# Masks made by GpSimd, score tiles in runs, and a new order of the first loads in an attention and max-out kernel

## The chip, the cores and the metric

The kernel runs on one core of a Trainium2 chip. The metric is the device time of one execution in microseconds (us). Three timed runs of the kernel before gave 184.52, 184.63 and 184.64, so the median is 184.63.

## What is computed

There are 4 batches of 8 heads, 768 positions and 64 elements per head. The reference in short:

```python
scores = scale * np.matmul(q, k.transpose(0, 1, 3, 2))
stream_keep = causal & (is_sink | in_win)     # 4 sinks, window 64
mask = where(is_retrieval[head], causal, stream_keep)
a = softmax(where(mask, scores, -1e9))
x = matmul(a, v)                              # heads side by side: (3072, 512)
h1, h2 = x @ w1, x @ w2                       # (512, 1024) each
out = np.maximum(h1, h2) @ w_out              # float32
```

Three of the eight heads see the whole causal triangle ("F"), five see only the sinks and the window ("S"). Which heads these are is data: the kernel reads the flags, sorts the heads and addresses them through registers.

## The kernel before, in words

The work is cut into 4 batches of two halves with 384 queries each, named (b, hf). Heads go in four pairs p: one FF, one FS and two SS.

For each half the stages are these. q, k and v are loaded as float32 by SyncE's queue (`load_half`, lines L513 and L523) into one of three large slots (`lds`). ScalarE, VectorE and GpSimd cast q and k to bf16 (`cast_qk`, helper lines L480 and L482). TensorE turns them (`turn`, L712), and a copy takes the result to SBUF (`unturn`). TensorE makes score tiles of two PSUM banks each (`scores`, L893). ScalarE takes the exponentials of each bank (`exp`, L912) into one of `NAT` = 6 tiles of weights. VectorE multiplies by 0/1 masks (`mask`, L931). TensorE multiplies the weights with v (`weighted`, L956), and VectorE divides by the row sums (`normalise`, L973 and L983). For the stream heads, `mix_k` and `mix_v` lay the sinks beside the window. The half (0, 0) differs: its masks come in as a bias of 0 or -1e30, added by a matmul with the identity ahead of the scores (L867, at most two in each score tile), so it needs no mask on VectorE.

max(h1, h2) is computed as relu(x(w1 - w2)) + x w2. So w1 - w2 goes to `w12` (VectorE, L1122, four column blocks c), and w2 w_out is made once: `P` turns w2 (L1138) and `P2` multiplies by w_out (L1156). P2 is 16 groups of two matmuls, named by block c and bank kc. Group c needs block c of w2, turned and copied out, and piece c of w_out, which GpSimd's queue loads and casts (L616). Each half then has eight `up` steps U (L1177, relus L1201 or L1203), each of four matmuls of 384 columns, and three output tiles D of twelve matmuls of 512 columns (L1227), which are copied out and stored by SyncE's queue (L1244). Batch 3 is loaded and cast by GpSimd's DMAs (L569) and turned by DMA (L583).

The order of the work is not written out by hand. A planner (class `Order`) plays the whole kernel through at build time with a cost for each operation, a rank for each kind (`RANK`), a minimum wait for some TensorE lists (`MARGIN`) and due times, and emits every engine's instructions in the order that it finds. On the chip each engine then follows this fixed order and waits on semaphores. TensorE takes from its lists in the order TX, W, S, TQ, P, H, P2, F. Where nothing is ready early on, the planner emits dummy matmuls on a zeroed tile (L471) to keep the clock up.

In the fixed order of before, SyncE's queue issues q and k of (0, 0), the bias table from HBM (L595, 256 KB), v of (0, 0), q and k of (0, 1), the four blocks of w2, v of (0, 1), the four blocks of w1, then batch 1. ScalarE's queue loads the flags (L1474) and the identity (L1558, 32 KB). VectorE makes the 0/1 tables from the bias table (L646). Score tiles are issued in fixed pairs (`TOGETHER`).

Of the kernel before, what the change touches and what calls it, by code (L numbers as in the profile page):

```python
# [39 lines left out]
def one(p, hh, blocks):  # L40
# [72 lines left out]
TOGETHER = (  # L113
    [[0, 1], [2, 3], [4, 5], [6]], [[0, 1], [2, 3], [4, 5], [6, 7], [8, 9]],
    [[0], [1], [2], [3], [4], [5]],
)
# [20 lines left out]
class Order:  # L137
# [6 lines left out]
    def __init__(self, banks, dummy, dummies_until):  # L144
        self.ops, self.lists, self.n, self.shift = [], {}, 0, 0.0
        self.banks, self.freed = [None] * banks, [0.0] * banks
        self.at, self.dummy, self.dummies_until = {}, dummy, dummies_until
# [41 lines left out]

    def run(self, names, allowed):  # L190
# [11 lines left out]
        rings, served = {"SP": [], "POOL": []}, [0.0, 0]  # L202
# [16 lines left out]
        def begin(o, e, t):  # L219
            cost = o.costs[e]  # L220
# [53 lines left out]
        left = len(self.ops)  # L274
        while events:
# [25 lines left out]
            while again:  # L301
# [20 lines left out]
                for relaxed in (False, True):  # L322
                    chosen = None
                    for n in names:
# [10 lines left out]
                        if o.claims and self.place(o.claims, False, SPARE.get(n, 0)) is None:  # L335
                            continue
                        chosen = n, o
                        break
                    if chosen:
# [4 lines left out]
                        begin(o, "PE", t)  # L344
                        again = True
                        break
                else:
                    if t < self.dummies_until:
                        spot = self.place([("dummy", 1)], False)
                        last = 0.107 if t < COLD_UNTIL else 0.056  # L350
                        if spot and (t < COLD_UNTIL or used(t) < WARM_SHARE):
                            self.dummy(spot["dummy"][0])
                            done_pe.append((t, t + last, 1.0))
                        if spot:
                            free["PE"] = t + last
                            push(t + last, None)
# [7 lines left out]
REGISTERS = 4.4  # L364
TURNED_BY_PE = (0,)
# [3 lines left out]
    'cast': 3.05, 'vcast': 13.85, 'unturn': 4.05, 'mix_k': -0.7, 'mix_v': -14.35, 'exp': 4.1,  # L369
    'mask': -5.1, 'norm': -4.75, 'take_x': -8.75, 'turn': 8.65, 'w2b': 9.4, 'sub': -4.6, 'w2t':  # L370
    -8.95, 'wob': -4.45, 'w2o': -10.4, 'relu': -0.25, 'load': 10.7, 'out': -0.6, 'h2': 7.85,
    'table': -2.75, 'vload': -2.25,
# [5 lines left out]
NAT = 6  # L378
# [19 lines left out]
W2O_EARLY = 3  # L398
# [3 lines left out]
DMA_LATE = {'SP': 2.7, 'POOL': 3.2}  # L402
RING = 4224
SPLIT = ((0, 0),)
K_BY_ACT = False
K_LANDS = 7.6
# [13 lines left out]
MARGIN = {'W': 2.0, 'S': 0.8, 'F': 2.0, 'TQ': 0.8}  # L420
X_MARGIN = 1.5


def tile_three_full_heads(
    tc, q, k, v, w1, w2, wo, out, tab, table_dram, heads, rez, found, verdict, warm, early_k, lds
# [18 lines left out]
    NLD, NQB, NQK, NMIX, NAT, NX, NXT, NG, NOUT = 3, 4, 8, 6, 6, 2, 4, 2, 4  # L444
# [33 lines left out]
    def copy(e, out, in_):  # L478
        if e == "ACT":
            nc.scalar.copy(out=out, in_=in_)  # L480
        else:
            eng[e].tensor_copy(out=out, in_=in_)  # L482

# [22 lines left out]
    def load_half(b, hf, kinds=(0, 1, 2)):  # L506
# [33 lines left out]
        if (b, hf) == (0, 0) and 0 in kinds:  # L540
            order_.insert(2 if long else 2 * NT, (3, 0))
        for t, i in order_:
# [3 lines left out]
            if t == 3:  # L546
                bias_in.append(load_table(128, 1152))
            elif t < 2 and long:
# [45 lines left out]
    def load_table(lo, hi):  # L594
        return dma(0.262, lambda _: nc.sync.dma_start(  # L595
            out=tab[:, lo:hi], in_=table_dram.ap()[:, lo:hi]
        ), rate=0.4, parts=128, grain=85.0)

# [25 lines left out]
    for what in LOADS:  # L624
        kind, c = what[:2], int(what[2:]) if what[:1] == "w" else 0
        if what[0] in "AB":
            kinds = (2,) if what[1:] else (0, 1)
            load_half(0, "AB".index(what[0]), kinds)
            flow += loads[0, "AB".index(what[0]), kinds[-1]]
# [6 lines left out]
    registers = order.given(REGISTERS)  # L636

# [143 lines left out]
    def prepare(b, hf, p):  # L781
# [7 lines left out]
        else:  # L789
# [4 lines left out]
            for hh in range(2):  # L794
                for lo, hi in ((0, 1), (1, 2)) if (b, hf) in SPLIT else ((0, 2),):
# [3 lines left out]
                        tag=f"cast{b}.{hf}.{p}", rank=RANK["cast"], port=("DVE", "POOL"),  # L799
# [9 lines left out]
            for hh in range(2) if b not in V_BY_DMA else ():  # L809
                vs.append(op(  # L810
                    dict(CAST_V), cast_v(n, hf, hh), [*loads[b, hf, 2], registers, *old_v],
                    tag=f"vcast{b}.{hf}.{p}", rank=RANK["vcast"], port=("POOL", "DVE"), bias=BIAS if b else None,
# [10 lines left out]
            else:  # L823
# [4 lines left out]
                    frees=[key], tag=f"unturn{b}.{hf}.{p}", rank=RANK["unturn"],  # L828
# [3 lines left out]
        if "S" in kind and (b or hf):  # L832
# [11 lines left out]
            for what in range(2) if hf == 0 or late else (1,):  # L844
                cols = 64 * (NT if hf else NT - 1 if what else 2 * NT - 1)
                ks.append(op({"DVE": 0.07 + cols / 1920}, mix_k(n, hf, what), [un, *firsts, *olds], tag=f"mixk{b}.{hf}.{p}", rank=RANK["mix_k"], port=("DVE",)))
                cols = VW * wide * (NT if hf else NT - 1 if what else 2 * NT - 1)
                vmix.append(op({"DVE": 0.045 + cols / 2400, "POOL": 0.25 + cols / 1200, "ACT": act(cols)}, mix_v(n, hf, what), [*vs, *vfirsts, *oldw], tag=f"mixv{b}.{hf}.{p}", rank=RANK["mix_v"], port=("POOL", "DVE"), bias=BIAS_MIX))
# [145 lines left out]
    def attend(b, hf):  # L994
        group = group_of(b, hf)
        exps, done = {}, {}
        for together in TOGETHER[2 if (b, hf) == (0, 0) else hf]:
            deps = []
            cost = 0.19
            for t in together:  # L1000
                blocks = [x_ for bk in group[t][0] for x_ in bk]
                for p, hh, blk in blocks:
# [6 lines left out]
                heads_ = [{(p, hh) for p, hh, _ in bk} for bk in group[t][0]]  # L1009
                serial = all(h[1] == 0 for s_ in heads_ for h in s_)  # L1010
                cost += mm(*[128] * len(group[t][0][0])) * (2 if serial else 1)
                cost += mm(*[128 * m * times for _, _, m, _, times in biases(b, hf, t)])
# [601 lines left out]
```

## Time and profile before

| | us |
|---|---|
| median of three timed runs | 184.63 |
| the profiled execution | 184.92 |
| its span, first to last instruction | 182.0 |
| TensorE busy, as the page counts it | 171.5 |
| ScalarE busy | 131.6 |
| VectorE busy | 96.7 |
| GpSimd busy | 42.4 |

The profiled execution is 2.9 us longer than its span, and 0.3 us longer than the median. TensorE's clock was granted at 0.998 of full speed. Matmuls are pipelined and their ends are modelled, so the busy time of TensorE contains overlaps: a group of 8 U matmuls is listed with 1.46 us, while the next group starts 1.3 us after it. Distances between starts are therefore used as costs, not the durations.

### The profile page before, as it was taken

To read this page: it belongs to the slowest core of one execution; us is meant where nothing else is said; L and a number is where in the kernel's file an instruction comes from. 1 tells how busy PE (TensorE), PEld (TensorE's weight loads), DVE (VectorE), ACT (ScalarE), POOL (GpSimd) and SP (SyncE) were. 2 spreads that over 40 slices of the span, in tenths; PEclk is the share of its full clock that TensorE was granted. 3 is DMA by queue.
4 is the path that set the end of the run, shared out by engine and by line. 5 is a ranking of instruction groups with operands and counts; after the bars stand their busy time and mean duration, and the time that the engine had idled before them with its cause. 6 is when DMAs were issued, how large, how long until landed. Compare 5 with 4: busy or idle time off the path is not lost.

```text
span 182.0 us, 4932 instructions
## 1 busy us (share of the span) xinstructions
PE 171.5 (94%) x1836; PEld 105.3 (58%) x1836; DVE 96.7 (53%) x283; ACT 131.6 (72%) x287; POOL 42.4 (23%) x77
## 2 busy tenths in 40 slices
PE   7599599989999999999999999999999999999991
PEld 7567486466647656565545565565466545545560
DVE  3356896599689984576247476656447500000000
ACT  3399794596899999999996984777797524525430
POOL 1000810100609489899580000000000000000000
PEclk9999999999999999999999999999999999999999
DMA  4999999999899999999999994160151052012022
GB/s 136 323 242 339 347 223 244 349 290 280 221 290 270 326 294 295 160 243 202 179 140 147 248 177 118 63 144 0 61 144 61 0 144 115 11 58 115 0 99 87
DMA packets 74930, 32.68 MB, mean 180 GB/s; under 512 B 54162, under 2 KB 71826, under 8 KB 74898
## 3 DMA queue, kind: packets, MB, share of 16 engines
q1 hardware_dynamic: 54848, 28.84, 62.4%
q0 software_dynamic: 19904, 3.41, 25.4%
q8 instruction: 16, 0.26, 0.6%
q14 instruction: 16, 0.13, 0.2%
q10 hardware_dynamic: 146, 0.03, 0.1%
HBM read 25.46 MB, written 6.29 MB: 174 GB/s over the span
## 4 chain that ended last, share of the span: by engine, by line
PE 64%; SPq 11%; DMA 9%; DVE 5%; ACT 4%; issue 2%; POOL 2%; POOLq 0%; DVEq 0%; ACTq 0%
PE ps L1227 30%; PE ps L1177 20%; DMA ld<-in_v_dram 6%; PE ps L956 6%; PE ps L893 6%; SPq L523 5%; SPq L608 3%; DMA ld<-in_q_dram 3%; DVE w L1122 2%; SPq L513 2%; PE ps L712 2%; ACT at L912 2%; ACT qk L480 1%; POOL qb L482 1%; DVE at L931 1%
## 5 line engine op out<-in xcount | busy, mean ns | idle before, releaser
L912 ACT ACTIVATE at<-ps 128x512 bf16<-128x512 f32 (+2 forms) x134 | 65.1, 601 | 3.5 <-PE ps L893 1.9
L1227 PE MATMUL ps<-wob,g 128*128 128x512 bf16 (+1 forms) x200 | 46.8, 371 | 0.2 <-ACT at L912 0.2
L1177 PE MATMUL ps<-xt,w 128*128 128x384 bf16 x256 | 46.0, 326 | 0.9 <-DVE w L1122 0.7
L1177 PEld LDWEIGHTS <-w 128*128 128x128 bf16 x256 | 23.6, 97 | 15.9 <-issue 0.9
L931 DVE TENSOR_TENSOR at<-at,tab 128x1024 bf16<-128x1024 bf16 (+5 forms) x49 | 25.6, 538 | 13.3 <-ACT at L912 13.0
L1201 ACT ACTIVATE g<-ps 128x384 bf16<-128x384 f32 x56 | 27.5, 504 | 7.0 <-PE ps L1177 6.5
L1227 PEld LDWEIGHTS <-g 128*128 128x128 bf16 x200 | 18.2, 98 | 17.8 <-issue 0.4
L480 ACT COPY ot<-ps 128x512 f32<-128x512 f32 (+1 forms) x20 | 11.4, 572 | 22.8 <-PE ps L1227 22.6
L1227 PE MATMUL ps<-w2o,xt 128*128 128x512 bf16 (+1 forms) x100 | 24.8, 371 | 0.3 <-ACT qk L480 0.3
L956 PEld LDWEIGHTS <-at 128*128 128x128 bf16 x477 | 19.9, 97 | 7.3 <-issue 0.2
L983 DVE TENSOR_TENSOR x<-ps,rez 128x192 f32 x64 | 22.8, 356 | 1.8 <-DVE x L983 0.2
L956 PE MATMUL ps<-vb,at 128*128 128x65 bf16 x387 | 21.6, 193 | 0.0
L482 POOL CAST qb<-ld 128x384 bf16 x23 | 12.1, 561 | 35.6 <-DMA ld<-in_k_dram 35.6
L893 PE MATMUL ps<-qk 64*128 64x128 bf16 (+1 forms) x322 | 20.2, 230 | 0.0
L893 PEld LDWEIGHTS <-qk 64*128 64x128 bf16 x322 | 12.0, 94 | 11.2 <-issue 8.2
L1227 PEld LDWEIGHTS <-xt 128*128 128x128 bf16 x100 | 9.2, 98 | 9.0 <-issue 0.5
L712 PE MATMUL ps<-tab,qb 128*128 128x128 bf16 x144 | 10.4, 219 | 4.0 <-DVE qb L482 2.1
L480 ACT COPY qk<-ps 128x768 bf16<-128x768 bf16 x17 | 12.9, 816 | 0.6 <-PE ps L712 0.6
L480 ACT CAST qb<-ld 128x384 bf16 (+1 forms) x23 | 8.8, 453 | 6.1 <-DMA ld<-in_k_dram 3.7
L471 PE MATMUL ps<-warmer 128*128 128x128 bf16 x147 | 11.0, 236 | 1.1 <-POOL warmer L1552 1.1
L712 PEld LDWEIGHTS <-qb 128*128 128x128 bf16 x144 | 8.3, 98 | 5.0 <-ACT qb L480 2.3
L471 PEld LDWEIGHTS <-warmer 128*128 128x128 bf16 x147 | 9.8, 107 | 1.4 <-POOL warmer L1552 1.1
(62 smaller groups left out, 145.5 us busy)
## 6 DMA issues: line engine op xcount, KB each, us to landing
out_dram<-ot SPq DMA_DIRECT2D x23, 256.0 KB, 2.1
ld<-in_q_dram SPq DMA_DIRECT2D x6, 768.0 KB, 7.0
ld<-in_k_dram SPq DMA_DIRECT2D x6, 768.0 KB, 7.4
ld<-in_v_dram SPq DMA_DIRECT2D x18, 256.0 KB, 6.7
ld<-in_moe_w_dram SPq DMA_DIRECT2D x8, 512.0 KB, 8.2
wob<-in_moe_w_out_dram POOLq DMA_DIRECT2D x4, 256.0 KB, 8.1
ld<-in_q_dram POOLq DMA_DIRECT2D x8, 96.0 KB, 6.6
ld<-in_k_dram POOLq DMA_DIRECT2D x8, 96.0 KB, 6.7
```

Of the source, the lines that this page charges most:

```text
L471: nc.tensor.matmul(banks[e][:, 0:128], lhsT=warm, rhs=warm, start=True, stop=True)
L480: nc.scalar.copy(out=out, in_=in_)
L482: eng[e].tensor_copy(out=out, in_=in_)
L712: nc.tensor.transpose(to[:, i], qbs[:, T["qb", n, hf] % NQB, t, i].rearrange("p h d -> p (h d)"), ident)
L893: nc.tensor.matmul(to.rearrange("p (i c) -> p i c", c=128), lhsT=lhsT, rhs=q_of(n, i, m)[rows], start=bk not in under, stop=True, skip_gro ...
L912: nc.scalar.activation(out=at[:, bk, 0:w], in_=bank(("ps", b, hf, t), part=bk)[:, 0:w], func=ACT.Exp, scale=scale,)
L931: eng[e].tensor_tensor(out=at, in0=at, in1=tbl, op=ALU.mult)
L956: nc.tensor.matmul(po[:, hh, i - NT * hf, :], lhsT=ats[:, T["at", b, hf, t] % NAT, bk, e * 128:(e + 1) * 128], rhs=rhs, start=first, stop= ...
L983: nc.vector.tensor_tensor(out=xs[:, (2 * b + hf) % NX, :, bass.ds(heads[2 * p + hh], 1), :], in0=po[:, hh, :, 0:D].unsqueeze(2), in1=z[:, ...
L1177: nc.tensor.matmul(bank(key)[:, 0:HALF], lhsT=w[:, kc, fc * 128:(fc + 1) * 128], rhs=xts[:, (2 * b + hf) % NXT, :, kc, :], start=(kc == 0) ...
L1201: nc.scalar.activation(out=g, in_=ph, func=ACT.Relu)
L1227: nc.tensor.matmul(bank(key)[:, cols], lhsT=lhsT, rhs=(w2o if kind == "x" else wob)[:, c, cols], start=(e == 0), stop=(e == len(steps) - 1),)
```

## The change

1. The bias table and the identity are no longer loaded. VectorE clears `tab`, then GpSimd writes the identity and the eight masks by eight selects and two copies. An instruction that reloads GpSimd's library index stands ahead of the first select in the built program. The planner assumes that the masks are there at 6.5 us.
2. The load order is q, k of (0, 0), q, k of (0, 1), v of (0, 0), then w2 in blocks 1, 3, 2, 0, v of (0, 1), then w1 in blocks 0, 3, 1, 2.
3. Score tiles are separate operations, but the planner starts a run of them only with at least two ready, counts 0.1 us for entering and 0.11 for leaving a run, and prefers to continue a run.
4. There are eight tiles of weights instead of six, and P2 goes bank by bank (`W2O_EARLY` = 0).
5. The very last half store is issued by ScalarE's queue.
6. Ranks, margins and rates of the planner are set anew, with ranks of their own for the two halves of batch 0.

The reserve program (`tile_any_heads`), which doesn't run with these inputs, is changed as well. The buffer `ok` of the closing test goes into a slot of `lds`.

```diff
+    def run_of_scores(self, first, t):
+        mine = self.lists["S"][first:]
+        mine = [o for o in mine if o.tag[1:3] == mine[0].tag[1:3]]
+        n = 1 if self.stuck or mine[0].tag[1:3] == (0, 0) else min(S_RUN, len(mine))
+        if len(mine) - n == 1 and not self.stuck:
+            n += S_REST
+        if any(o.left or o.ready > t + 1e-9 for o in mine[:n]):
+            return False
+        return sum(e is None for e in self.banks) >= 2 * n
...
-                    for n in names:
+                    for n in ("S", *names) if last == "S" else names:
...
+                        if n == "S" and last != "S" and not self.run_of_scores(at[n], t):
+                            continue
...
+                        extra = ENTER_S if n == "S" and last != "S" else LEAVE_S if last == "S" and n != "S" else 0.0
...
+MASKS_MADE = 6.5
-NAT = 6
+NAT = 8
-    'A', 'Av', 'B', 'w23', 'wo0', 'wo1', 'wo2', 'w20', 'wo3', 'w21', 'w11', 'w10', 'w12', 'w22',
-    'w13', 'Bv',
+    'A', 'B', 'Av', 'w21', 'wo0', 'wo1', 'w10', 'w23', 'w13', 'w11', 'w12', 'w22', 'wo2', 'wo3',
+    'w20', 'Bv',
-BIAS = {'DVE': 1, 'ACT': 0}
+BIAS = {'DVE': 0, 'ACT': 1}
-W2O_EARLY = 3
+W2O_EARLY = 0
+LAST_BY_ACT = True
-RATE = {'first': 0.3, 'long': 0.34, 'v': 0.27, 'w': 0.36, 'wo': 0.37, 'cast': 0.22}
+RATE = {'first': 0.26, 'long': 0.32, 'v': 0.25, 'w': 0.355, 'wo': 0.37, 'cast': 0.22}
-STEP = 2.4
-FF_STEP = -2.1
+STEP = 2.95
+FF_STEP = 0.5
+S_RUN = 2
+S_REST = 1
+ENTER_S = 0.1
+LEAVE_S = 0.11
-MARGIN = {'W': 2.0, 'S': 0.8, 'F': 2.0, 'TQ': 0.8}
-X_MARGIN = 1.5
+MARGIN = {'W': 0.5, 'S': 0.2, 'F': 1.2, 'TQ': 0.8}
+X_MARGIN = 2.5
...
-        for together in TOGETHER[2 if (b, hf) == (0, 0) else hf]:
+        for t in range(len(group)):
...
+                    (nc.scalar if ends else nc.sync).dma_start(
...
+def mask_table(nc, bias, n_sink, window):
+    at = lambda i, n=1: bias[:, 128 * i:128 * (i + n)]
+    def put(i, n, base, by_key, by_query, fill=-1e30):
+        nc.gpsimd.affine_select(
+            out=at(i, n).rearrange("p (n c) -> p n c", c=128), in_=at(i, n).rearrange("p (n c) -> p n c", c=128),
+            pattern=[[0, n], [by_query, 128]], compare_op=ALU.is_ge, fill=fill, base=base,
+            channel_multiplier=by_key,
+        )
+    put(7, 1, 0, -1, 1)
+    put(0, 1, n_sink - 1, -1, 0)
+    put(1, 2, window - 129, 1, -1)
+    put(2, 1, -n_sink, 1, 0, 0.0)
+    put(3, 3, window - 1, 1, -1)
+    put(3, 1, -n_sink, 1, 0, 0.0)
+    put(3, 3, 0, -1, 1)
+    nc.gpsimd.tensor_copy(out=at(6)[0:64], in_=at(0)[0:64])
+    nc.gpsimd.tensor_copy(out=at(6)[64:128], in_=at(1)[64:128])
...
+        nc.vector.memset(tab[:, 0:1152], 0.0)
+        nc.gpsimd.affine_select(
+            out=tab[:, 0:128], in_=tab[:, 0:128], pattern=[[1, 128]], compare_op=ALU.not_equal, fill=1.0,
+            base=0, channel_multiplier=-1,
+        )
+        mask_table(nc, tab[:, 128:1152], n_sink, window)
...
-        nc.scalar.dma_start(out=tab[:, 0:128], in_=table_dram.ap()[:, 0:128])
```

The order that the planner makes of it, read from the two built programs (TQ turns q and k, TX turns x):

| TensorE | before | after |
|---|---|---|
| ahead of the last dummies (in before one single dummy more comes behind W) | both TQ, S tiles 0 to 3 of (0, 1), TX of (0, 0), first P | both TQ, S tiles 0 to 6 of (0, 1), all P, two groups of P2 |
| between the last P2 and the first U | W of (0, 1), 46 matmuls, then a pair of S | none (59 matmuls of W stand ahead of the last three groups of P2) |
| dummies in all | 147 | 177 |
| runs of S after the first U | 25 | 21 |

On GpSimd six casts of v of (0, 0) stand ahead of the four w_out loads, where two casts of q and k of (0, 1) stood. On VectorE the four table instructions stand ahead of the casts of the first k; seven of the eight q and k casts of (1, 0) are VectorE's (none before), with four of its v casts behind them.

More of the change, by code (lines that the diff above doesn't have):

```diff
@@ L368 @@
 RANK = {
[L369 to L372, printed above, removed]
+    'cast': 4.8, 'vcast': 9.75, 'unturn': 3.75, 'mix_k': -3.75, 'mix_v': -11.35, 'exp': 6.3,
+    'mask': -6.4, 'norm': -3.65, 'take_x': -9.8, 'turn': 9.2, 'w2b': 10.05, 'sub': -5.05, 'w2t':
+    -9.85, 'wob': -5.05, 'w2o': -12.95, 'relu': -3.3, 'load': 11.6, 'out': -2.75, 'h2': 3.75,
+    'table': -0.9, 'vload': -2.45,
 }
@@ L401 @@
 DMA_FIRST = 1.95
-DMA_LATE = {'SP': 2.7, 'POOL': 3.2}
+DMA_LATE = {'SP': 2.7, 'POOL': 3.2, 'ACT': 2.2}
 RING = 4224
@@ new lines, in attend @@
+            exps[t] = list(both_)
+            for part in group[t][1] if (b, hf) not in BIASED else ():
+                cols = 128 * part[1] * part[3]
+                exps[t].append(op(
+                    {"DVE": 0.07 + cols / 1920}, mask(b, hf, t, part),
+                    both_[part[0]:part[0] + part[1]] + table_in, tag=f"mask{b}.{hf}.{t}", rank=rank_of("mask", b, hf, t), port=("DVE",),
+                ))
+            done[t] = mine
+            for p in range(HP):
+                if used(b, hf, t, p):
+                    last_s.setdefault(b * HP + p, []).append(s)
@@ L1248, in forward @@
                 )
+                if ends:
+                    op({"ACT": 0.5}, store, [ev], data=0.000512 * width_ / 0.38, grain=85.0)
+                    continue
                 ot_free[number].append(
```

215 lines of the change are left out of this document (99 added, 116 removed).

## The prediction

> **What bounds the kernel now.** I read the page first, then TensorE's timeline, then the list of what TensorE waited for.
>
> ```profile
> span 182.0 us, 4932 instructions
> PE   7599599989999999999999999999999999999991
> DMA  4999999999899999999999994160151052012022
> GB/s 136 323 242 339 347 223 244 349 290 280 221 290 270 326 294 295 160 243 202 179 140 147 248 177 118 63 144 0 61 144 61 0 144 115 11 58 115 0 99 87
> ```
>
> A slice is 4.55 us. The DMA engines are full from the second slice on, and TensorE shows gaps only in the first 35 us, where part of its work is dummies besides.
>
> ```profile
> 25.96 0.50 PE L471 MATMUL ps<-warmer 128*128 128x128 bf16 x6
> 26.40 0.28 PE L893 MATMUL ps<-qk 64*128 64x128 bf16 x3
> 30.40 5.79 PE L1156 MATMUL ps<-wob,w2t 128*128 128x512 bf16 x26
> 36.02 1.23 PE L956 MATMUL ps<-vb,at 128*128 128x65 bf16 x35
> 38.86 3.42 PE L1177 MATMUL ps<-xt,w 128*128 128x384 bf16 x20 [0.67 <-DVE w L1122]
> ```
>
> At 26.40 the last row of dummies ends. From there TensorE has real work in stock, up to the first U at 38.86 and on to the end. What it waited for from 38 to 90 us is this; from 90 to 180 the view lists nothing:
>
> ```profile
> PE ps L1177 <- DVE w L1122: 0.7, 1, 0.7
> PE ps L1227 <- ACT qk L480: 0.3, 1, 0.3
> PE ps L1177 <- ACT qk L480: 0.3, 1, 0.3
> PE ps L1227 <- ACT at L912: 0.2, 1, 0.2
> ```
>
> These are 1.5 us in 140. So the end is the moment at which the stock begins, plus the stock. A change gains by fitting more real work ahead of that moment, by making the stock itself cheaper, or by removing a share of the 1.5 us. Cheaper work on another engine gains nothing.
>
> **Runs of scores.** These pieces of the chain price the entering and leaving of a run:
>
> ```profile
> 109.51 0.55 PE ps L893 x16
> 114.02 0.44 PE ps L893 x12
> 115.92 0.86 PE ps L1227 x4
> 117.22 0.97 PE ps L1227 x4
> ```
>
> Four more score matmuls cost 0.11, so one costs 0.0275, and 12 of them should take 0.33. They take 0.44: entering costs 0.11. The D group that follows other work takes 0.86, the one behind a run 0.97: leaving costs 0.11. In the built order 25 runs follow the first U, then 21. Four runs at 0.22 are **-0.9 us** from the stock, and nothing covers them, as TensorE is the bound there. The runs ahead of the first U count in the next part.
>
> **The new order of the front.** After the change TensorE's last dummies stand ahead of the third group of P2 of the first bank. That group needs piece 2 of w_out and block 2 of the turned w2. First w_out:
>
> ```profile
> 18.99 1.24 POOL L482 CAST qb<-ld 128x384 bf16 x2 [14.28 <-DMA ld<-in_k_dram]
> 20.18 3.17 POOL L616 DMA_DIRECT2D wob<-in_moe_w_out_dram  x4
> DMA to landing us min/median/max: 6.8/8.1/9.6
> 48.07 1.22 POOL L482 CAST vb<-ld 128x192 bf16 x4
> ```
>
> The third row belongs to the four issues of the second. They come 0.79 apart, so the third begins at 21.77; as third of four it lands between the median and the longest, I take 8.6, so 30.4. After the change the 256 KB table isn't ahead of it: at 323 GB/s (second slice) that is 0.8 us less DMA work. The last of the first q, k, v and second q, k lands 0.8 earlier, near 18.1 (v now, k before). GpSimd then makes six v casts of 0.305 (last row), 1.8 us, where two casts took 1.2. The issue stays near 20.0, and the DMA backlog puts the landing at 29.6, with 29.1 to 30.6 as bounds (8.1 and 9.6).
>
> Next the other need, ScalarE's chain:
>
> ```profile
> 23.59 5.82 ACT L912 ACTIVATE at<-ps 128x512 bf16<-128x512 f32 x12
> L480 ACT COPY qk<-ps 128x768 bf16<-128x768 bf16 x17 | 12.9, 816 | 0.6 <-PE ps L712 0.6
> ```
>
> W of (0, 0) waits for v (18.1 plus 1.8), the first run of S takes 0.44, so exponentials of (0, 1) start at 20.4, 3 us ahead of the first row. Fourteen at 0.485 end at 27.2, and the copy of w2's block 2 (as the second row, a third wider) at 28.1 or so. So w_out decides, with 1.5 us to spare.
>
> From 29.6 I add up to the first U: third group 0.43, 24 scores 0.88, TX of 12 at 0.056 (0.67; next fence), ten groups of P2 at 0.43 (26 matmuls from 30.40 to 36.02 are 0.216 each), 59 W at 0.03 (1.8), three groups (1.3). That is 39.0. But 13 W (0.4) are then done that before came later, so it compares with 38.6 against 38.86: **-0.25 us**, bounds -0.75 and +0.75.
>
> ```profile
> 47.54 0.83 PE L1086 MATMUL ps<-tab,x 128*128 128x128 bf16 x12
> 48.21 1.50 PE L712 MATMUL ps<-tab,qb 128*128 128x128 bf16 x24
> 96.14 0.24 PE ps L956 x8
> 36.45 3.48 DVE L1122 TENSOR_TENSOR w<-ld 128x1024 bf16<-128x1024 f32 x3
> ```
>
> The first U also needs w1 - w2 of block 0, second in line before and first now; at 1.2 us each VectorE is done with it near 37, so the 0.7 wait goes and TensorE's own work is late next.
>
> **Masks by GpSimd.** These are the nearest rows:
>
> ```profile
> 0.85 0.20 POOL L1552 MEMSET warmer<- 128x128 bf16 x1 [0.29 <-POOLq L1595]
> 4.29 0.42 POOL L464 MEMSET vb<- 128x384 bf16 x1 [3.23 <-DVE warm L1559]
> 8.55 0.87 DVE L482 CAST qb<-ld 128x192 bf16 x3 [1.32 <-DMA ld<-in_k_dram]
> 9.34 0.62 DVE L646 TENSOR_SCALAR tab<-tab 128x128 bf16<-128x128 bf16 x4
> tab<-mask_table ACTq DMA_DIRECT2D x1, 32.0 KB, 4.9
> ```
>
> The two memsets give 0.1 us plus 0.85 ns a column. Ten operations over 1920 columns are 2.6 us by that, 3.1 if each is as slow as a cast (0.305 for 192 columns, less overlap). With the clearing on VectorE ahead of them the masks are there at 4.7. The trace shows no select and no library reload. Below, the reload is free; above, it waits for two fetches, one after the other, as long as the small table's (4.9 each): 13.9. One fetch gives 9.1. Who waits: VectorE's four table instructions (0.62), and behind them the casts of k, which land at 8.55. Up to 7.9 nothing is late. Later masks push scores, exponentials and w2's copy, which have 1.5 us to spare. So the cost is 0 up to 9.4 and one for one from there. I take **0**.
>
> The Trainium skill speaks against this: the page "GPSIMD Engine Reference", section "Instruction dispatch", gives the first call of a freshly loaded kernel an IRAM load of about 6 us that no profile row shows. As an estimate by that figure the masks come at 10.1 and the sum below is 0.7 less; no run here shows such a load yet.
>
> **The rest.** VectorE now casts q and k of (1, 0), and that has a place where it is late:
>
> ```profile
> 46.19 1.75 ACT L480 CAST qb<-ld 128x384 bf16 x4 [1.28 <-DMA ld<-in_k_dram]
> 18.93 0.94 DVE L482 CAST qb<-ld 128x384 bf16 x2 [0.75 <-DMA ld<-in_k_dram]
> 51.89 1.06 DVE L482 COPY kx<-qk 64x320 bf16<-64x320 bf16 x6 [0.22 <-ACT qk L480]
> ```
>
> k lands near 45.4 (0.8 earlier). Seven casts at 0.47, four v casts, two unturns, two v mixes and four of six k mixes put the third run's k mix at 53.1; TensorE arrives at 52.5. That is a wait of 0.6 where 0.2 was: **+0.4**, bounds 0 and 1.5. Eight weight tiles, P2 by banks and smaller margins cost no instruction. They change waits only: bounds -1.5 (all listed waits gone) and, with 1.5 us less margin for W in six halves, +9. The rows of 0.2 to 0.3 are nearer to nothing: 0.
>
> ```profile
> 178.08 0.37 ACT L480 COPY ot<-ps 128x256 f32<-128x256 f32 x1 [0.89 <-PE ps L1227]
> L1244 SPq DMA_DIRECT2D out_dram<-ot x25: 332/333/1700, 50.4 to 178.5; - x25
> 1.41 0.38 ACTq L1558 DMA_DIRECT2D tab<-mask_table  x1
> ```
>
> The last copy ends at 178.45, SyncE issues the store at 178.5. ScalarE saves at most those 0.05 and issues as slowly (0.38 against 0.33): **0**, bounds -0.05 and +0.05.
>
> The sum: -0.9 - 0.25 + 0.4 = **-0.75 us**. The profiled execution would go from 184.92 to 184.2; the median of the three runs lies 0.29 below it, so I predict **183.9**.
>
> **The rivals.**
>
> Masks late. The place is VectorE's table instructions, which stand ahead of the casts of k. If the reload takes one and a half of the small fetches (7.35), the masks come at 1.05 + 7.35 + 3.1 = 11.5 and cost 2.1: 186.0, slower. It decides from 10.1, where it eats the gain. For it speaks that the reload's code has to be fetched while the DMA engines are full; against it that even one whole fetch of 4.9 costs nothing, and that ScalarE has 1.5 us of cover.
>
> A reload of little over one fetch, with masks at 10.1: cost 0.7, time 184.6, so the masks and the table's load cancel. In that case the change doesn't do what it says for the front. This is where the page's figure lies.
>
> Thin margins. TensorE's order is fixed, and W may now stand 0.5 us behind its planned weights instead of 2.0. If ScalarE or VectorE runs 0.5 late once in each of six halves, that is +3.0: 186.9. For it: ScalarE is filled to nine tenths in the middle of the span:
>
> ```profile
> 75.00:80.00 5.00, 5.00 (x63) 3.10 (x58) 3.22 (x8) 4.98 (x12) 5.00 (x8) 1.00 1.78 231
> ```
>
> (columns: TensorE, its weight loads, VectorE, ScalarE 4.98 of 5 us, GpSimd). Against it: one wait moves all that follows, so the next weights are no longer late, and eight weight tiles let ScalarE run ahead.
>
> Larger gain. If w_out's piece 2 lands as fast as its first (6.8), the third group could go at 27.8, ScalarE's chain then limits it to 28.1, 1.5 earlier. Without the wait at (1, 0) either, the sum is -0.9 - 0.25 - 1.5 = -2.65: 182.0.
>
> **How the numbers follow.** I give the forecast 0.44, late masks 0.14, masks at 10.1 0.10, thin margins 0.16, the larger gain 0.16. About 0.37 us (0.2%) is what a measurement of this kernel can tell from no change. The forecast's own bounds (the front's -0.75 to +0.75, the wait's 0 to 1.5) give 183.0 to 186.0 with most of it under 184.3: of its 0.44 I count 0.33 faster, 0.08 same, 0.03 slower. The larger gain is faster; masks at 10.1 split 0.03, 0.05, 0.02; late masks 0.01 same, 0.13 slower; thin margins 0.01, 0.02, 0.13. Together: faster 0.53, same 0.16, slower 0.31. The range runs from 0.5 under the larger gain to the thin margins' price, 181.5 to 187.0; two fetches of masks (188.4) and the margins' far end are left out. Faster and slower both hold much, so the forecast's own range stands beside it: 183.0 to 184.6.
>
> **What would show it.** Right: the masks' last GpSimd instruction ends before 9.4; the third P2 group starts at 29 to 30.6 and the first U near 39.0; from there to TensorE's end there are about 138.3 us instead of 139.2; a wait of 0.3 to 1 us stands ahead of a score run near 53; the tail from the last matmul is unchanged. Wrong: table instructions on VectorE that start after 9.4; a first U after 40 with w_out long landed (then ScalarE's chain was the limit); waits of TensorE from 55 to 140 that sum to over 1 us; fewer than 21 runs' worth of saving, seen as D groups that still take 0.97.

## The result, and the profile after

The changed kernel takes 189.18 us (median of four runs, 188.0 to 189.88) against 184.63 for the kernel before in the same comparison: a ratio of 1.0244, 95% interval 1.0207 to 1.0281. It is slower by 4.5 us, above the range of the prediction.

The profiled execution took 188.97 us with a span of 187.4, 5.4 more than before. The lines have moved: L738 turns q and k (L712 before), L510 casts, L598 issues the loads of batch 3 (L569), L920 is S, L983 W, L1173 P2, L1194 U, L1244 D, L499 the dummies. From the page of the kernel after:

```profile
span 187.4 us, 4980 instructions
PE   7999997999999999999944999999999999999992
PEclk9999999999999999999995699999999999999999
```

A slice is 4.7 us. Slices 21 and 22 (94 to 103 us) have TensorE at four tenths, and slices 22 and 23 have its clock at half and at six tenths: neither hole exists before. What TensorE waited for from 40 us to the end is this (total, times, longest):

```profile
PE ps L738 <- POOL qb L510: 4.9, 1, 4.9
PE ps L1244 <- issue: 0.5, 3, 0.2
```

One wait, and it is for a cast by GpSimd. TensorE's timeline around it (start, length):

```profile
94.67 0.50 PE L738 MATMUL ps<-tab,qb 128*128 128x128 bf16 x6
95.01 1.03 PE L1244 MATMUL ps<-wob,g 128*128 128x512 bf16 x4
100.92 0.82 PE L738 MATMUL ps<-tab,qb 128*128 128x128 bf16 x6 [4.88 <-POOL qb L510]
...
103.30 0.82 PE L738 MATMUL ps<-tab,qb 128*128 128x128 bf16 x6
103.91 1.49 PE L1194 MATMUL ps<-xt,w 128*128 128x384 bf16 x4
```

The turn of the second pair of (2, 1) starts 4.88 us late. Behind it six turns take 0.82 instead of 0.50 and four U matmuls 1.49 instead of 0.81. The windows show why. Columns: TensorE, its weight loads, VectorE, ScalarE, GpSimd, then the granted clock, the DMA engines' share and GB/s.

```profile
98.50:99.00 0.50, 0.00 (x0) 0.00 (x0) 0.00 (x0) 0.00 (x0) 0.00 (x0) 1.00 1.38 235
99.00:99.50 0.50, 0.00 (x0) 0.00 (x0) 0.00 (x0) 0.00 (x0) 0.43 (x1) 0.56 1.61 147
...
105.80:106.20 0.40, 0.40 (x6) 0.27 (x4) 0.00 (x0) 0.26 (x2) 0.00 (x0) 0.89 1.07 186
```

The clock falls to one half at about 99.06 (0.56 over half a microsecond: seven eighths of it at half speed), 3 us after TensorE went idle, and comes back at about 105.89, 5 us after it resumed.

Why did the cast come so late? Its data were there: SyncE issued k of (2, 1) at 68.39, and the four loads of q and k that it issued from 50 to 110 us landed within 7.6 us.

```profile
68.39 2.30 SPq L546 DMA_DIRECT2D ld<-in_k_dram  x1
DMA to landing us min/median/max: 6.8/7.3/7.6
```

GpSimd's timeline shows what stood ahead of it, all 24 loads of batch 3:

```profile
69.68 1.65 POOL L598 DMA_DIRECT2D vb<-in_v_dram  x2 [4.13 <-PE ps L983]
...
78.12 0.82 POOL L598 DMA_DIRECT2D ld<-in_q_dram  x1 [0.71 <-DMA vb<-in_v_dram]
80.35 0.82 POOL L598 DMA_DIRECT2D ld<-in_k_dram  x1 [1.41 <-DMA vb<-in_v_dram]
...
82.43 0.82 POOL L598 DMA_DIRECT2D ld<-in_q_dram  x1 [0.63 <-DMA ld<-in_q_dram]
84.61 0.82 POOL L598 DMA_DIRECT2D ld<-in_k_dram  x1 [1.36 <-DMA ld<-in_k_dram]
...
99.07 0.82 POOL L598 DMA_DIRECT2D vb<-in_v_dram  x1 [2.45 <-DMA ld<-in_k_dram]
99.94 0.35 POOL L510 COPY vx<-vb 64x204 bf16<-64x204 bf16 x1
100.36 0.50 POOL L510 CAST qb<-ld 128x384 bf16 x1
```

An issue takes 0.82 us, but from the 13th load on nearly each one first waits for a landing, and where it does, the releaser is the load eight places ahead in this queue: the two v loads for the 13th and 14th, a q for the 15th, a k for the 16th. So at most eight of these loads are under way, and GpSimd stands still meanwhile. The pace is then the larger of 0.82 and an eighth of the time to landing. Median times to landing, from the page of after and, in the window 50 to 120, of before (KB each, us to landing):

```profile
ld<-in_q_dram POOLq DMA_DIRECT2D x8, 96.0 KB, 11.9
ld<-in_k_dram POOLq DMA_DIRECT2D x8, 96.0 KB, 12.6
```

```profile
ld<-in_q_dram POOLq DMA_DIRECT2D x8, 96.0 KB, 6.6
ld<-in_k_dram POOLq DMA_DIRECT2D x8, 96.0 KB, 6.7
```

6.6 over eight is 0.83, just what an issue takes: before, GpSimd waits for only one of these landings (1.66 us at 89.47). 12 over eight is 1.5, and the loads that the 13th to the 20th wait for took longer than the median: the last of them was issued at 76.54 and landed at 91.91. So these issues come 2.08 apart (78.12 to 92.68). GpSimd's waits for landings add up to 11.4 us from the 13th load on. Without them, as an estimate, the cast would have ended near 89.5, and TensorE ran out of work at 96.04. Why the loads land so much later than before, no run here isolates; with the casts moved ahead the medians are 12.8 and 12.5, so TensorE's wait isn't the reason.

The planner charges 0.85 for an issue (`CAST_ISSUE`) and knows nothing of the eight places, so the order that it found has no room for this. In the order before, GpSimd's casts of q and k of (2, 1) stand between the first loads and end at 76.9.

The front went much as forecast (timelines of after):

```profile
1.72 0.29 POOL L1590 TENSOR_SCALAR_AFFINE_SELECT tab<-tab 128x128 bf16<-128x128 bf16 x1 [0.60 <-DVE tab L1589]
1.97 2.69 POOL L1540 TENSOR_SCALAR_AFFINE_SELECT tab<-tab 128x128 bf16<-128x128 bf16 x7
4.95 0.29 POOL L1553 COPY tab<-tab 64x128 bf16<-64x128 bf16 x1
30.09 0.59 PE L1173 MATMUL ps<-wob,w2t 128*128 128x512 bf16 x2 [1.02 <-DMA wob<-in_moe_w_out_dram]
39.48 2.11 PE L1194 MATMUL ps<-xt,w 128*128 128x384 bf16 x12
183.89 0.37 ACT L508 COPY ot<-ps 128x256 f32<-128x256 f32 x1 [0.89 <-PE ps L1244]
```

The masks are made at 5.24, the third group of P2 starts at 30.09 and waits for w_out, the first U stands at 39.48. From the first U to the start of the last copy there are 144.41 us, against 139.22 before (38.86 to 178.08); from there to the end of the span 3.51, against 3.92. So the 5.4 us are +0.62 in the front, +5.19 in the stock and -0.41 in the tail. The front's share is uncertain: in four more kernels whose front has the order of after, the first U stands between 39.04 and 39.96. The stock holds a wait of 4.88 and the half clock, so without these it has become shorter.

### The profile page after: what moved, and what is told of

The parts are those of the page before. It is cut to its first block, busy times and chain, and to the rows that moved or that the text cites. A ratio compares the mean times of both kernels' runs of the same rounds, so it can differ in the third digit from the quotient of the medians.

```text
span 187.4 us, 4980 instructions
## 1 busy us (share of the span) xinstructions
PE 174.6 (93%) x1846; PEld 110.6 (59%) x1866; DVE 100.1 (53%) x300; ACT 129.8 (69%) x275; POOL 42.5 (23%) x83
## 3 DMA queue, kind: packets, MB, share of 16 engines
q0 software_dynamic: 19904, 3.41, 23.7%
## 4 chain that ended last, share of the span: by engine, by line
PE 67%; DMA 16%; issue 5%; SPq 5%; POOL 4%; POOLq 0%; DVE 0%; ACT 0%
PE ps L1244 27%; PE ps L1194 20%; DMA ld<-in_k_dram 7%; PE ps L983 7%; PE ps L920 6%; DMA wob<-in_moe_w_out_dram 5%; DMA ld<-in_v_dram 4%; PE ps L1173 3%; PE ps L738 3%; SPq L546 3%; SPq L556 2%; POOL vb L510 1%; POOL vb L598 1%; POOL wob L640 1%; PE ps L1103 1%
## 5 line engine op out<-in xcount | busy, mean ns | idle before, releaser
L939 ACT ACTIVATE at<-ps 128x512 bf16<-128x512 f32 (+2 forms) x134 | 65.2, 585 | 10.1 <-PE ps L920 9.4
L1244 PE MATMUL ps<-wob,g 128*128 128x512 bf16 (+1 forms) x194 | 46.6, 370 | 0.6 <-issue 0.5
L1194 PE MATMUL ps<-xt,w 128*128 128x384 bf16 x256 | 46.6, 329 | 0.0
L958 DVE TENSOR_TENSOR at<-at,tab 128x1024 bf16<-128x1024 bf16 (+5 forms) x49 | 24.8, 517 | 19.3 <-ACT at L939 18.8
L1194 PEld LDWEIGHTS <-w 128*128 128x128 bf16 x256 | 24.0, 99 | 15.0 <-issue 0.5
L1218 ACT ACTIVATE g<-ps 128x384 bf16<-128x384 f32 x53 | 26.1, 500 | 7.3 <-PE ps L1194 7.1
L508 ACT COPY ot<-ps 128x512 f32<-128x512 f32 (+1 forms) x22 | 12.8, 580 | 23.5 <-PE ps L1244 22.7
L1244 PEld LDWEIGHTS <-g 128*128 128x128 bf16 x200 | 17.9, 98 | 17.1 <-issue 0.2
L1244 PE MATMUL ps<-w2o,xt 128*128 128x512 bf16 (+1 forms) x89 | 23.9, 369 | 0.6
L983 PEld LDWEIGHTS <-at 128*128 128x128 bf16 x477 | 19.9, 98 | 6.9 <-issue 0.4
L983 PE MATMUL ps<-vb,at 128*128 128x65 bf16 x387 | 21.6, 194 | 0.0
L920 PE MATMUL ps<-qk 64*128 64x128 bf16 (+1 forms) x322 | 20.2, 234 | 0.1
L920 PEld LDWEIGHTS <-qk 64*128 64x128 bf16 x322 | 12.3, 95 | 9.0 <-issue 5.8
L508 ACT COPY qk<-ps 128x768 bf16<-128x768 bf16 x16 | 12.8, 832 | 6.4 <-PE ps L738 6.3
L738 PE MATMUL ps<-tab,qb 128*128 128x128 bf16 x144 | 11.7, 231 | 5.1 <-POOL qb L510 4.9
L499 PE MATMUL ps<-warmer 128*128 128x128 bf16 x177 | 14.4, 248 | 1.8 <-POOL warmer L1588 1.2
L1244 PEld LDWEIGHTS <-xt 128*128 128x128 bf16 x100 | 9.5, 98 | 9.3
L499 PEld LDWEIGHTS <-warmer 128*128 128x128 bf16 x177 | 13.0, 114 | 2.7 <-POOL warmer L1588 1.2
L738 PEld LDWEIGHTS <-qb 128*128 128x128 bf16 x144 | 9.5, 103 | 7.8 <-POOL qb L510 5.4
L1000 DVE RECIPROCAL rez<-ps 128x6 f32<-128x6 f32 x32 | 5.5, 196 | 15.1 <-PE ps L983 15.0
L510 DVE CAST qb<-ld 128x384 bf16 (+1 forms) x31 | 10.0, 374 | 4.2 <-DMA ld<-in_k_dram 3.2
## 6 DMA issues: line engine op xcount, KB each, us to landing
ld<-in_k_dram POOLq DMA_DIRECT2D x8, 96.0 KB, 12.6
```

The costliest lines, as they stand in the source:

```text
L499: nc.tensor.matmul(banks[e][:, 0:128], lhsT=warm, rhs=warm, start=True, stop=True)
L738: nc.tensor.transpose(to[:, i], qbs[:, T["qb", n, hf] % NQB, t, i].rearrange("p h d -> p (h d)"), ident)
L920: nc.tensor.matmul(to.rearrange("p (i c) -> p i c", c=128), lhsT=lhsT, rhs=q_of(n, i, m)[rows], start=bk not in under, stop=True, skip_gro ...
L939: nc.scalar.activation(out=at[:, bk, 0:w], in_=bank(("ps", b, hf, t), part=bk)[:, 0:w], func=ACT.Exp, scale=scale,)
L958: eng[e].tensor_tensor(out=at, in0=at, in1=tbl, op=ALU.mult)
L983: nc.tensor.matmul(po[:, hh, i - NT * hf, :], lhsT=ats[:, T["at", b, hf, t] % NAT, bk, e * 128:(e + 1) * 128], rhs=rhs, start=first, stop= ...
```

## The experiments

Times of one group were taken on one chip beside the kernel before. For most variants the planner's list is kept and only rearranged:

```diff
-            o.emit(e)
+            plan.append((e, o))
...
+        for e, o in reorder(plan):
+            o.emit(e)
```

### First group: the wait, the clock, the tail, the runs (before: 184.26)

**casts_ahead**

```diff
+    for what, load, n in (("cast2.1.", "load3.3", 0), ("vcast2.1", "load3.2", 4)):
+        late = [x for x in plan if mine(x, what)]
+        plan = [x for x in plan if x not in late]
+        at = [i for i, x in enumerate(plan) if mine(x, load)][n]
+        plan = plan[:at] + late + plan[at:]
```

> The changed kernel with one thing moved: on GpSimd's list alone, the two casts of q and k and the six casts of v for the second part of the third batch stand ahead of the last loads of the fourth batch instead of behind all 24 of them. Every other engine has the same order. Theory (GpSimd's order): the wait of 4.9 us ahead of the second turn of that part goes, and with it the stretch of about 5 us behind it in which the granted clock was 0.50, worth some 2.4 us; the time falls from 189.0 to about 181.7, TensorE waits under 0.5 us between 90 and 110, and the clock is 1.00 there. Rival (the clock drops by itself): the wait goes, a stretch at half clock stays somewhere: 184.1. Rival (thin margins): the next late operation stands right behind and takes the wait over: above 187.

182.47 us, ratio 0.9907 (0.988 to 0.9934). From 40 us on no wait of TensorE is listed, and the first turn of (2, 1) stands where it stood in after, with the other three behind it by 98.48, all at full speed:

```profile
94.69 0.50 PE L738 MATMUL ps<-tab,qb 128*128 128x128 bf16 x6
...
98.48 0.50 PE L738 MATMUL ps<-tab,qb 128*128 128x128 bf16 x6
```

```profile
39.49 2.11 PE L1194 MATMUL ps<-xt,w 128*128 128x384 bf16 x12
176.92 0.37 ACT L508 COPY ot<-ps 128x256 f32<-128x256 f32 x1 [0.89 <-PE ps L1244]
```

(The same kernel: first U and last copy.) The stock is 137.43 us, 6.98 less than in after, by moving eight casts on one queue. GpSimd's order as the cause holds; "thin margins" falls, for nothing took the wait over.

**dummies_in_wait**

```diff
+    return plan[:at] + [("PE", ("pt", 9, 1))] * 84 + plan[at:]
```

> The changed kernel with 84 dummy matmuls of 128 columns (about 4.6 us of TensorE) ahead of the turn that waits 4.9 us for GpSimd's cast; the wait itself stays filled, nothing else moves. Theory (the clock is lost because TensorE stood idle): the granted clock stays at 1.00 from 95 to 110, the work behind the wait runs at full speed, and the time falls by about 2.4 us, to 186.6. Rival (the clock drops by itself, or through a dense stretch before): still 0.50 for about 5 us, 189.0 or more.

186.97 us, ratio 1.0145 (1.0117 to 1.0174). TensorE's one wait there is now short, and the clock is whole:

```profile
PE ps L738 <- POOL qb L510: 0.5, 1, 0.5
```

```profile
95.00:100.00 5.00, 5.00 (x85) 4.75 (x84) 1.50 (x4) 1.64 (x4) 2.84 (x5) 1.00 1.66 135
100.00:105.00 5.00, 4.51 (x62) 3.23 (x60) 3.13 (x12) 3.61 (x7) 2.99 (x9) 1.00 1.64 234
```

The stock is 142.46 (39.04 to 181.50), 1.95 less than in after, with the cast as late as ever (100.2). So idleness lowers the clock, not the density of the work before, and the 7 us of after divide into about 4.9 of waiting and 2.0 to 2.1 of half speed.

**casts_ahead_sync_store**

```diff
-LAST_BY_ACT = True
+LAST_BY_ACT = False
```

> The kernel with the casts ahead, and the very last store (256 columns) issued by SyncE as in the kernel before instead of ScalarE. Expectation from the two traces (3.5 us from the end of the last copy to the end of the span before, 3.1 after): 0.35 us slower than the kernel with the casts ahead. My prediction's step gave this part nothing (at most 0.05): then the same time.

183.59 us, ratio 0.9959 (0.9937 to 0.9981). In this profile the first U stands at 39.84 and the last copy starts at 177.06, so the stock is 137.22, as with the casts ahead. From that copy to the end of the span (181.4) there are 4.34 us, against 3.88 (176.92 to 180.8). With SyncE's store the kernel before shows 3.92, with ScalarE's the kernel after 3.51. Each pair says 0.4 to 0.5 us, but these distances scatter as much: with ScalarE's store they go from 3.43 (the kernel with the casts elsewhere, below) to 3.88 and more. The issue itself is a cleaner row (before, then after):

```profile
178.48 0.86 SPq L1244 DMA_DIRECT2D out_dram<-ot  x1
184.29 0.38 ACTq L1263 DMA_DIRECT2D out_dram<-ot  x1
```

The last issue takes SyncE 0.57 to 0.89 us in the three profiles with its store, and ScalarE 0.38 at most in the eleven others. From the start of the issue to the landing there are 2.2 to 2.6 us with SyncE and 1.7 to 2.1 with ScalarE. So ScalarE's store does gain, by some tenths of a microsecond. The medians differ by 1.1; 0.35 of that is the later front of this profile, and what else they hold stays open.

**casts_ahead_split_runs**

```diff
+            if score(plan[a][1]) and score(plan[b][1]) and group(plan[c][1]) and not any(x[1] in deps for x in plan[b:c]):
+                plan[b:c + 1] = [plan[c]] + plan[b:c]
```

So S S D becomes S D S, six times.

> The kernel with the casts ahead, and six of its runs of scores cut in two by putting the next group of four D matmuls ahead of the run's last scores: 30 runs of scores instead of 24, the same matmuls. If entering and leaving a run costs TensorE 0.22 us, as the prediction has it: 1.3 us slower than with the casts ahead. If the 0.11 seen at each end is only how the pipelined durations are counted, or is hidden: 0 to 0.3 us slower.

183.88 us, ratio 0.9986 (0.9963 to 1.0009). First U and last copy:

```profile
39.96 2.11 PE L1194 MATMUL ps<-xt,w 128*128 128x384 bf16 x12
178.24 0.37 ACT L508 COPY ot<-ps 128x256 f32<-128x256 f32 x1 [0.89 <-PE ps L1244]
```

A stock of 138.28, 0.85 longer: 0.14 for each of the six runs (27 instead of 21 behind the first U). In the five kernels here with the casts ahead and the same order of the stock it lies between 137.07 and 137.45, so the price is 0.14 to 0.20. Entering and leaving a run does cost TensorE time, but less than the 0.22 that I read from the chain's pieces. Of the 1.4 between the medians, 0.47 is the front of this profile: the third group of P2 starts between 29.65 and 30.57 in kernels whose front is the same. The rest stays open.

### Second group: another way round, and the front (before: 184.61)

A difference of two ratios is uncertain by 0.7 to 1 us (half widths of 0.003 to 0.0045, taken together).

**casts_elsewhere**

```diff
-                    dict(CAST_V), cast_v(n, hf, hh), [*loads[b, hf, 2], registers, *old_v],
+                    {k_: c_ for k_, c_ in CAST_V.items() if k_ != 'POOL' or (b, hf) != (2, 1)}, cast_v(n, hf, hh), [*loads[b, hf, 2], registers, *old_v],
```

(and the same for `CAST_QK`)

> The changed kernel with one rule more in its planner: the casts of the second part of the third batch may not go to GpSimd, so they stand on VectorE and ScalarE; the fourth batch's 24 loads keep GpSimd's list as it was. Theory (it was the place behind the loads, nothing about that cast itself): no wait of TensorE over 0.5 us from 90 to 110 and the time of the kernel with the casts ahead, 182.5, within 0.4. Rival (ScalarE and VectorE have no room there, which is why the planner used GpSimd): exponentials and masks come late, TensorE waits some 1 to 2 us, 183.5 or more.

182.9 us, ratio 0.9911 (0.9872 to 0.9951), and of TensorE's waits after 40 us only the three of 0.2 for its own issue are left. It was the place, not the cast, and one rule in the planner is enough. This and the kernel with the casts ahead are the fastest here; every version that is faster than the kernel before, clear of noise, has these casts out of that place.

**masks_loaded**

```diff
-        nc.vector.memset(tab[:, 0:1152], 0.0)
...
-        mask_table(nc, tab[:, 128:1152], n_sink, window)
+        nc.scalar.dma_start(out=tab[:, 0:128], in_=table_dram.ap()[:, 0:128])
+        HELD[:] = [lambda _: nc.sync.dma_start(out=tab[:, 128:1152], in_=table_dram.ap()[:, 128:1152])]
...
+    return plan[:sp] + [("SP", SimpleNamespace(emit=HELD[0], deps=[], tag=None))] + plan[sp:]
```

> The kernel with the casts ahead, with identity and masks loaded again as in the kernel before (32 KB by ScalarE's queue, 256 KB by SyncE's between k of the first part and q of the second) instead of made by GpSimd; every engine's order is otherwise the same. Theory (the front ends with the landing of the third piece of w_out, and the DMA engines are full until then): 0.8 us of DMA work more puts that group of P2 near 30.9 and the first U 0.8 us later: 183.3. Rival (the table's load is hidden, as each queue goes at its own pace): third group and time unchanged, 182.5.

183.67 us, ratio 0.9949 (0.9923 to 0.9975), 0.8 above the kernel with the casts ahead by the ratios. v, w_out and the third group are all later by about 0.8:

```profile
18.34 1.79 POOL L510 CAST vb<-ld 128x192 bf16 x6 [13.64 <-DMA ld<-in_v_dram]
20.08 2.97 POOL L640 DMA_DIRECT2D wob<-in_moe_w_out_dram  x4
30.94 0.59 PE L1173 MATMUL ps<-wob,w2t 128*128 128x512 bf16 x2 [0.34 <-DMA wob<-in_moe_w_out_dram]
```

So 288 KB less in a full front is worth about 0.8 us, as the prediction's front step had it. The first U stands at 40.32, against 39.04 to 39.96 in the five kernels with the same front and made masks, so the 0.8 could be 0.4 to 1.3.

**masks_late**

```diff
+        for _ in range(12):
+            nc.gpsimd.memset(tab[:, 1152:1664], 0.0)
         mask_table(nc, tab[:, 128:1152], n_sink, window)
```

> The kernel with the casts ahead, with twelve memsets of 512 columns on GpSimd (about 6.4 us, into columns that are written later anyway) between the identity and the masks, so that the masks end near 11.6 instead of 5.2. The prediction's rule (nothing up to 9.4, one for one from there): 2.2 us slower, 184.7, with the first U near 41.7. Rival (the front has more cover than I gave it, since TensorE runs dummies until w_out's third piece is there): 0 to 0.7 us slower. Other rival (no cover at all): more than 4 us.

186.7 us, ratio 1.012 (1.0075 to 1.0164), 3.9 above the kernel with the casts ahead.

```profile
11.81 0.29 POOL L1553 COPY tab<-tab 64x128 bf16<-64x128 bf16 x1
13.14 2.40 PE L738 MATMUL ps<-tab,qb 128*128 128x128 bf16 x21 [5.04 <-DVE qb L510]
34.49 0.60 PE L1173 MATMUL ps<-wob,w2t 128*128 128x512 bf16 x2
```

The masks end at 12.1, so the rule "one for one from 9.4" gives 2.7. Then there is the clock again: TensorE stood idle for 5.04 us, and its 21 turns take 2.40 where they take 1.33 in after: 1.07 more, 3.8 with the 2.7. In the trace the third group comes 4.39 later than with the casts ahead (30.10), so 0.6 of that stays open. "More cover" falls. "No cover", which was priced at over 4, isn't excluded by the time; but the masks are 6.9 later and the front only 4.4, so part of it was covered.

**w_out_ahead**

```diff
+    at = [i for i, x in enumerate(plan) if mine(x, "vcast0.0")][2]
+    return plan[:at] + wo + plan[at:]
```

> The kernel with the casts ahead, with the four issues of w_out on GpSimd's list ahead of four of the six v casts that they stood behind: they are issued about 1.2 us earlier, those casts come about 3 us later. Theory (TensorE's front ends with the landing of w_out's third piece): the third group of P2 starts 0.5 to 1.2 us earlier and the first U with it: 181.5 to 182.0. Rival (the v casts are on the way to the weights of the first part, so ScalarE's and VectorE's chain becomes the bound): 0.5 us or more slower than with the casts ahead.

184.43 us, ratio 0.9989 (0.9961 to 1.0017): 1.5 slower than with the casts ahead, so the rival was right.

```profile
18.42 2.97 POOL L640 DMA_DIRECT2D wob<-in_moe_w_out_dram  x4
21.80 1.55 PE L983 MATMUL ps<-vb,at 128*128 128x65 bf16 x40 [2.57 <-POOL vb L510]
31.79 0.61 PE L1173 MATMUL ps<-wob,w2t 128*128 128x512 bf16 x2
```

The first weights wait 2.57 us for v, and the third group comes at 31.79 without any wait for w_out. TensorE's own list ahead of that group, dummies included, ends at most 1.1 us before w_out lands: so long is the longest wait at that group in the kernels with the same front, and in the one with dummies in the wait there is none. Dummies stand in the fixed order like all else: a late start pushes them back and isn't absorbed by them.

### Third group: parts undone, planned again (before: 184.33)

These three start from the kernel with the casts kept off GpSimd (0.9911). The planner finds a new order each time, with ranks that were set for the change, so they tell what a part is worth in that company, not by itself.

**margins_back**

```diff
-MARGIN = {'W': 0.5, 'S': 0.2, 'F': 1.2, 'TQ': 0.8}
-X_MARGIN = 2.5
+MARGIN = {'W': 2.0, 'S': 0.8, 'F': 2.0, 'TQ': 0.8}
+X_MARGIN = 1.5
```

> The kernel with the casts kept off GpSimd (182.9), planned again with the margins of the kernel before (2.0 us for weights, 0.8 for scores, 2.0 for U and D groups, 1.5 for the first U of a part, in place of 0.5, 0.2, 1.2 and 2.5). If thin margins cost anything beside the one wait for GpSimd, the time falls below 182.5. My theory (they cost nothing, as TensorE waits under 1 us in all from the first U on): 182.9 to 184.5, the loss being work that the planner holds back.

184.67 us, ratio 1.0004 (0.9975 to 1.0034), 1.7 slower. In that company the thin margins gain; beside the one wait for GpSimd they did not cost.

**six_tiles**

```diff
-NAT = 8
+NAT = 6
```

> The kernel with the casts kept off GpSimd, planned again with six tiles of weights instead of eight. The prediction gave the two more tiles nothing: then 182.9, within 0.4. Rival (the tiles let ScalarE run ahead, and that is why TensorE no longer waits): ScalarE's exponentials wait for free tiles, TensorE waits 1 to 2 us more in all, 184 to 185.

186.27 us, ratio 1.0101 (1.0057 to 1.0146), 3.5 slower. Its first U stands at 38.92 and its last copy at 178.87, a stock of 139.95 against 137.29 with the casts kept off GpSimd (39.38 to 176.67), while its listed waits are three of 0.4 to 0.5. Of the 2.66 more, 24 score matmuls and 22 W that stand behind the first U here and ahead of it there are about 1.5 (0.88 and 0.66 by the prediction's prices). From the last copy to the end of the span there are 5.23 us instead of 3.43, although the last store lands at 180.99, as quickly as there: 1.8 us of this profile that no tile of weights explains. Eight tiles are worth more than nothing; what in the new order costs the rest isn't settled.

**v_before_q_k**

```diff
-    'A', 'B', 'Av', 'w21', 'wo0', 'wo1', 'w10', 'w23', 'w13', 'w11', 'w12', 'w22', 'wo2', 'wo3',
+    'A', 'Av', 'B', 'w21', 'wo0', 'wo1', 'w10', 'w23', 'w13', 'w11', 'w12', 'w22', 'wo2', 'wo3',
```

> The kernel with the casts kept off GpSimd, planned again with the load order of the kernel before at that place (v of the first part ahead of q and k of the second). By the prediction's front step the order by itself is worth little: the landing of w_out's third piece ends the front either way, so 182.9, within 0.5, plus 0.15 for each of the three runs of scores that this plan has more: 183.4. Rival (q and k early are what lets ScalarE's chain end before w_out lands): first U over 1 us later, 184 or more.

189.97 us, ratio 1.0294 (1.0252 to 1.0336), 7.1 slower, by both theories too much. GpSimd got no v casts of the first half in this plan and issues w_out at 6.15 us, ahead of everything that the front needs first. The first cast of v starts at 17.62, as late as in after (17.63), although SyncE issues v from 2.05 on instead of 5.9. That w_out's 1 MB ahead of it is the reason is likely, not shown. The first weights wait, and the clock falls once more:

```profile
6.15 2.99 POOL L640 DMA_DIRECT2D wob<-in_moe_w_out_dram  x4
18.12 1.06 PE L983 MATMUL ps<-vb,at 128*128 128x65 bf16 x16 [3.95 <-DVE vb L510]
45.13 1.46 PE L1194 MATMUL ps<-xt,w 128*128 128x384 bf16 x8
```

It is no measure of the load order; it shows the same kind of accident as the change itself.

**before_q_k_ahead** (the kernel before, with the opposite edit)

> The kernel before with one part of the change alone: q and k of the first batch's second part loaded ahead of the first part's v, all else planned as before. By the prediction's front step: 0 to 0.3 us faster than the kernel before (184.6). Rival (v later makes the first weights later, and nothing else profits): 0.5 to 0.8 us slower.

185.48 us, ratio 1.0053 (1.0019 to 1.0087): 1.0 slower; its first U stands at 39.59 instead of 38.86. By itself the order costs, as the rival said (0.35 to 1.6 by the interval). Whether the 0.62 by which the front of after is late comes from it isn't shown.

## Why the prediction was wrong

Taken in its own order:

- **The bound.** Right: the end is the first U plus the stock, in every run here, with a tail of 3.4 to 5.2 us behind them.
- **Runs of scores, -0.9.** Right in kind; at 0.14 to 0.20 a run the four are -0.6 to -0.8.
- **The front, -0.25.** The third group does wait for w_out (30.09, said 29.6), the first U stands at 39.48 (said 39.0), inside the bounds. The larger gain, with that group at 27.8, did not come. But "1.5 us to spare" on ScalarE's chain was wrong as a reserve of the front: the list of TensorE itself is as good as late.
- **Masks, 0.** Right: 5.24, under 9.4. The first select, of 128 columns, takes 0.29, the seven others 2.69 together, and no reload shows. The Trainium skill's 6 us ("GPSIMD Engine Reference", section "Instruction dispatch") is not seen: the first select follows the clearing by VectorE at 1.72.
- **The wait at (1, 0), +0.4.** It did not come, nor did the 0.8 us of other waits behind the first U that before shows.
- **"Eight weight tiles, P2 by banks and smaller margins cost no instruction. They change waits only ...: 0."** This step failed. The new plan also moved GpSimd's queue, which I read in batch 0 and not in batches 2 and 3. There it put a cast that TensorE needs behind 24 loads: 4.88 us of wait and 2.1 of half clock, 7.0 in all. Which of the planner's new constants put it there, no run here shows. The sign "waits of TensorE from 55 to 140 that sum to over 1 us" came true. The bound of +9 contained it, but for another reason (late weights, six times over), and I chose 0 by the nearest rows. In the built order that cast stood last but for its fellows; the landing of 6.6 us against eight places, in the trace of before, and the one wait of 1.66 there, would have told that those loads had no slack at all.
- **The tail, 0.** -0.4 in the two profiles. My 0.33 for SyncE's issue was the median of all 25 stores; the last one took 0.86, and ScalarE's 0.38.

Without the misplaced cast the stock is 1.79 shorter than before (137.43 against 139.22): 0.6 to 0.8 for the runs, 0.8 for the waits that went, and 0.4 for the 13 W that now come ahead of the first U add up to about that. Median against median it is -1.8, where I had said -0.75. The rivals: late masks and masks at 10.1 fall; "thin margins" had the right shape (a fixed order in which something came late) with the wrong engine, the wrong count and no price for the clock.

## What to carry to other kernels

When a planner's constants change, compare the built order of every engine over the whole kernel, and for each instruction that TensorE waits on ask what is queued ahead of it and whether that can stall. With at most eight loads under way, GpSimd's issues went at the pace of the landings here (2.08 us instead of 0.82), and everything behind them stood still, casts included. A wait of TensorE can cost more than its length: the 4.88 us in the middle of the stock cost 7.0, and the 5.04 us of the kernel with late masks slowed the turns behind them by another 1.07.

## What the hardware showed beside that

- **The clock follows idleness in steps.** In three kernels TensorE stood idle for 3.95, 4.88 and 5.04 us, and the clock was half for 6.8 us (16.24 to 23.06), 6.8 (99.06 to 105.89) and 3.4 (12.6 to 16.0). The idle 2.57 us of the kernel with w_out ahead left it at 1.00. These are the rows for the first, fall and return:

```profile
16.00:17.00 1.00, 0.00 (x0) 0.00 (x0) 0.00 (x0) 0.12 (x1) 0.00 (x0) 0.62 1.13 356
...
23.00:24.00 1.00, 1.00 (x24) 1.00 (x23) 0.93 (x4) 0.77 (x2) 0.00 (x0) 0.97 1.10 346
```

The Trainium skill, "TensorE: Matmul & The Clock Gate", section "What's actually happening", describes a free-running window of about 3.4 us in which an idle window halves the clock and a busy one restores it. The runs agree: each stretch at half clock is one or two such windows. But the window ahead of a fall need not be idle throughout: of the 3.41 us before the three falls, TensorE's timeline shows it busy for 0.40, 0.11 and 0.00 (as shares, in the order above). Of the two windows over which the 2.57 us lay, reckoned from that trace's clock edges, it was busy for 0.65 and 0.60.

- **At most eight of GpSimd's loads were under way**, and the ninth issue held GpSimd until the landing of the first. The trace of after shows the form of the wait: these issues wait on eight semaphores in turn (numbers 114 to 121), each raised by the load eight places ahead. So the wait stands in the built program; whether the chip has a limit of its own behind it, no run here tells.
